# Where the weights' rounding copies and the softmax division run in the first groups of an attention and feed-forward kernel

## The chip, the cores and the metric

One NeuronCore of a Trainium2 chip runs the whole kernel. The metric is the device time of one execution in microseconds. Five engines work side by side, each with its own queue of instructions in a fixed order: TensorE (PE, its weight loads PEld), VectorE (DVE), ScalarE (ACT), GpSimd (POOL) and SyncE (SP), which issues nearly all transfers.

## What is computed

Attention with a local and a global window over 4 batches, 8 heads, 768 positions and 64 dimensions, then a feed-forward layer from 512 to 2048 and back.

```python
scores = scale * np.matmul(q, k.transpose(0, 1, 3, 2))
is_global = pos[None, :] < int(n_global)                 # 8
is_local = (rel >= 0) & (rel < int(n_local))             # 96
scores = np.where(is_global | is_local, scores + bias, -1000000000.0)
a = np.exp(scores - np.max(scores, axis=-1, keepdims=True))
a = a / (np.sum(a, axis=-1, keepdims=True) + 1e-09)
x = matmul(a, v)                                         # regrouped to 3072 rows of 512
h = x @ w_in                                             # w_in: 512 x 2048
g = np.where(h > 0.0, h, np.exp(np.minimum(h, 0.0)) - 1.0)
out = g @ w_out                                          # w_out: 2048 x 512
```

The two weight matrices arrive as 64-bit floats, as pairs of 32-bit words.

## The kernel before, in words

The 3072 rows are cut into 12 groups of 256 rows (`W`). Each group has four pairs of heads. For a pair, TensorE makes scores (`s`), DVE subtracts the distance table and takes the row maximum (L647, `pr`), ACT takes the exponential and sums it (L649), DVE adds 1e-9 and inverts the sums (`st`, L662 and L663), the scores are multiplied by the inverse (`norm`, by the helper `scaled`: L633 on ACT, L635 on DVE, L637 on POOL), TensorE transposes them (`t`), they are copied to SBUF (`pt`) and multiplied with the values (`pv`). The result is kept as a rounded part and a residual (`xh`, HI and LO). The groups 0 to 3 do this in `pair32`, where `norm` is called with `both=True`; the later groups do it in `pair`, with `both=False`.

The feed-forward layer has 16 blocks of 128 hidden units. TensorE makes `h` (L803), ACT and DVE make the ELU (`e`, L733 to L735), the result is rounded by ACT (`gh`) and its residual (`gl`) made by DVE or POOL, and TensorE multiplies it into the output (`o`, L763). Groups 0 to 2 go through the blocks in three segments, 0 to 4, 5 to 9 and 10 to 15, each for all three groups (`SEGS`). From group 3 on a scheme with seven products works on pairs of blocks (`a`, L880), with combinations of the second matrix's weights (`combos`, `g7`, L464, and `ta`, `tb`).

A weight block is prepared once, in `weight`, in the time of groups 0 to 2: SP loads the words (`bits`), ACT takes the absolute value of the high words (L433), DVE clamps, shifts and merges the words in four steps (L434, L438, L440, L442) into a 32-bit float (`g`), one copy rounds it to the type that TensorE reads (`w`, HI, by the helper `copy`: L336 on ACT, L338 on DVE and POOL), and one subtraction makes the residual (LO, L344, DVE or POOL). There are 32 such blocks, 16 of each matrix.

The order of all this work is not written by hand. Each operation is added to a `Plan` with a due time and a list of alternatives, each an engine, a cost in ns and whether it reserves the port that the planner lets DVE and POOL share. The planner runs through the work with these costs, and an operation goes to the engine where it would end first; what comes out is each engine's fixed queue. An operation that several engines may do is listed with several alternatives:

```python
def pool(n, two=True):
    return (("POOL", (30 + 2.58 * n) if two else (50 + 1.1 * n), True),)
```

`act`, `dve` and `pool` give these alternatives for n columns. A `dve` alternative reserves the port when it is marked fast or port.

Of the kernel before, what the change touches and what calls it, by code (L numbers as in the profile page):

```python
# [26 lines left out]
HI, LO = 0, 1  # L27
# [232 lines left out]
def act(n, psum=False, extra=0.0):  # L260
    return (("ACT", (55 if psum else 97) + 0.834 * n + extra, False),)


def dve(n, fast=False, port=False):
    return (("DVE", (75 + 0.521 * n) if fast else (70 + 1.042 * n), fast or port),)


def pool(n, two=True):
    return (("POOL", (30 + 2.58 * n) if two else (50 + 1.1 * n), True),)


def sp():
    return (("SP", 450.0, False),)


class Kernel:
# [136 lines left out]
    def weight(self, which, fc, due, after):  # L413
        nc, p, DM = self.nc, self.plan, self.DM
        tag = f"w{which}{fc}"
        bits = self.sb(tag, "bits", [P, 2 * DM], I32)
        g = self.sb("io", "g", [P, DM], I32)
        w = self.sb(tag, f"w{which}", [P, 2, DM], F32R)
        src = (self.w_in, self.w_out)[which][fc].bitcast(I32)
        words = lambda: bits.t.rearrange("p (n w) -> p n w", w=2)  # L420
        low, high = lambda: words()[:, :, 0], lambda: words()[:, :, 1]
        gf = lambda: g.t.bitcast(F32)

        def fetch(e):
            nc.sync.dma_start(bits.t, src)
            while self.values:
                self.values.pop(0)()

        load = p.add(sp(), fetch, writes=[bits], due=due - 9000, after=after, nbytes=P * DM * 8)
        if fc in self.ASKED:  # L430
            self.asked.append(load)
        if which in self.ABS:
            p.add((("ACT", 575.0, False),), lambda e: nc.scalar.activation(gf(), high().bitcast(F32), AF.Abs), [bits], [g], due - 6000)  # L433
            p.add(dve(DM, True), lambda e: nc.vector.tensor_scalar(gf(), gf(), F64_MIN, F64_MAX, ALU.max, ALU.min), [g], [g], due - 5500)  # L434
        else:
            p.add(dve(DM, port=True), lambda e: nc.vector.tensor_scalar(
                gf(), high().bitcast(F32), F64_MIN, F64_MAX, ALU.abs_max, ALU.min), [bits], [g], due - 5500)
        p.add(dve(DM, True), lambda e: nc.vector.tensor_scalar(g.t, g.t, 3, 0x3FFFFFFF, ALU.logical_shift_left, ALU.bitwise_and),  # L438
              [g], [g], due - 5000)
        p.add(dve(DM, port=True), lambda e: nc.vector.scalar_tensor_tensor(g.t, high(), -0x40000000, g.t, ALU.bitwise_and, ALU.bitwise_or),  # L440
              [bits, g], [g], due - 4500)
        p.add(dve(DM, port=True), lambda e: nc.vector.scalar_tensor_tensor(g.t, low(), 29, g.t, ALU.logical_shift_right, ALU.bitwise_or),  # L442
              [bits, g], [g], due - 4000)
        p.add(act(DM), lambda e: self.copy(e, w.t[:, HI], gf()), [g], [w], due - 3000)
        p.add(pool(DM) + dve(DM, port=True), lambda e: self.minus(e, w.t[:, LO], gf(), w.t[:, HI]),
              [g, w], [w], due - 2000)
        if which == 0 or fc < self.NF7:
            cols = slice(0, DM) if which == 0 else slice(DM // 2, DM)
            self.stores[which, fc] = p.add(sp(), lambda e: nc.sync.dma_start(self.kept[which][fc], w.t.bitcast(F32)[:, :, cols]), [w],
                                           due=due + self.KEEP, nbytes=P * DM * 8 // (1 + which), floor=self.KEEP)  # L450
        return w
# [30 lines left out]
    def pair(self, b, gi, hp, xh, xl, due, ahead, step, X):  # L482
# [41 lines left out]
        if rows:  # L524

            if "held" in X:
                self.loads += loads
            p.add((() if b == gi == 0 and hp < 3 else act(W) + dve(W, True)) + pool(W, False),
                  lambda e: self.scaled(e, q32(), q32(), sc), [rqv], [rqv], due - 9000)
            pv = self.bank("pv", "pv", [P, NT, P], X.get("pv"))  # L530
            self.pair32(b, hp, t0, q32, k32, v32, rqv, rk, pv, due, step, X)
            pvs = lambda: pv.t.rearrange("p i w -> p (i w)")
            p.add(act(W, True) + dve(W), lambda e: self.copy(e, xh.t[:, HI, hp], pvs()), [pv], [xh], due + 700)
            p.add(dve(W), lambda e: self.minus(e, xh.t[:, LO, hp], pvs(), xh.t[:, HI, hp]), [pv, xh], [xl], due + 800)
            if "held" in X:
                self.held += [o for v in (rqv, rk) for o in v.readers]
            return
# [132 lines left out]

    def norm(self, pr, lo, st, i, due, both):
        n = WN - lo
        more = act(n, extra=90) + pool(n, False) if both else act(n)
        self.plan.add(more + (("DVE", 130 + 0.53 * n, True),), lambda e: self.scaled(
            e, pr.t[:, lo:], pr.t[:, lo:], st.t[:, 2, i:i + 1]), [pr, st], [pr], due)

    def pair32(self, b, hp, t0, q32, k32, v32, rqv, rk, pv, due, step, X):
# [257 lines left out]
    def build(self):  # L935
# [46 lines left out]
        for fc, d in wdue.items():  # L982
            for which in range(2):
                def weight(which=which, fc=fc, d=d):
                    self.ws[which][fc] = self.weight(which, fc, d + 2 * which * self.STEP, self.loads + self.held if fc >= self.LATE else self.loads if fc > 1 else ())
                todo.append((first[fc] - 100.0, weight))
# [329 lines left out]
```

## Time and profile before

| | us |
|---|---|
| median of 3 runs | 657.6 (656.93 to 657.79) |
| the profiled execution, its own time | 655.9 |
| its span in the profile | 654.0 |
| busy in the span: PE, DVE, ACT, POOL | 641.9, 521.0, 478.1, 39.3 |
| POOL instructions in the span | 65 |

The profile is of one execution. An engine's busy time is the time in which it works on some instruction; the ends of matmuls are modelled, so a busy TensorE is not TensorE at its peak. The chain of work that ended last is followed back from the last instruction, at each step to what released it or to the instruction ahead of it on its engine. Rows of a group of instructions give the line, the engine, the operation, what is written and read with its shape, the count, the busy time and the mean length, and the idle time of the engine just before them.

### The profile page before, as it was taken

What the parts mean: (1) busy time and instruction counts of PE and PEld (TensorE: products, weight loads), DVE (VectorE), ACT (ScalarE), POOL (GpSimd) and SP (SyncE); (2) the same over time, 40 slices, a digit from 0 to 9 for tenths busy, and PEclk for the clock granted to TensorE, in tenths of its full rate; (3) what the DMA queues carried; (4) which work ended last, traced back from release to release, by engine and by line L of the source; (5) the groups of instructions that cost most, each with busy time, mean ns of one, the idle gap of its engine ahead of it and who ended that gap; (6) DMA issues with size and microseconds to landing.
All of it is one profiled execution on the core that took longest, in us unless ns stands there. A gap on an engine that the chain in (4) does not pass through costs nothing.

```text
span 654.0 us, 15999 instructions
## 1 busy us (share of the span) xinstructions
PE 641.9 (98%) x5950; PEld 599.0 (92%) x5950; DVE 521.0 (80%) x1510; ACT 478.1 (73%) x1243; POOL 39.3 (6%) x65
## 2 busy tenths in 40 slices
PE   8999999999999999999999999999999999999996
PEld 6677888888888999999999999999999999999996
DVE  7999999999998867866877786876777778766655
ACT  7998879766878777776777777776777777774442
POOL 4143101110211000000000000000000000000000
PEclk9999999999999999999999999999999999999999
DMA  8846996710237567657756756666775685575661
GB/s 272 302 119 221 365 361 248 275 65 13 73 112 262 191 215 241 237 190 233 254 190 213 274 180 223 237 234 202 229 263 181 222 284 187 178 250 174 216 204 36
DMA packets 52373, 137.71 MB, mean 211 GB/s; under 512 B 5698, under 2 KB 19010, under 8 KB 52290
## 3 DMA queue, kind: packets, MB, share of 16 engines
q1 hardware_dynamic: 52000, 136.37, 61.4%
q8 instruction: 48, 0.79, 0.5%
q14 instruction: 35, 0.29, 0.1%
q10 hardware_dynamic: 290, 0.26, 0.1%
HBM read 119.84 MB, written 16.78 MB: 209 GB/s over the span
## 4 chain that ended last, share of the span: by engine, by line
PE 83%; DVE 11%; ACT 3%; DMA 1%; issue 1%; POOL 0%; DVEq 0%; POOLq 0%; SPq 0%
PE h L803 36%; PE a L880 26%; PE o L763 6%; PE pv L614 4%; PE s L556 3%; PE t L576 3%; DVE g L464 2%; PE pv L725 1%; DMA rqv<-in_qkv_dram 1%; PE t L708 1%; ACT pr L649 1%; DVE gl L344 1%; PE s L691 1%; DVE e L735 1%; DVE g L440 1%
## 5 line engine op out<-in xcount | busy, mean ns | idle before, releaser
L803 PE MATMUL h<-xh,w0s 128*128 128x256 f32 x1728 | 203.1, 276 | 0.0
L803 PEld LDWEIGHTS h<-xh,w0s 128*128 128x128 f32 x1728 | 199.5, 188 | 0.1
L880 PE MATMUL a<-w,gg 128*128 128x256 f32 x864 | 143.5, 277 | 0.3 <-DVE xh L344 0.3
L336 ACT CAST gg<-z 128x384 fp32r<-128x384 f32 (+1 forms) x144 | 81.3, 565 | 70.4 <-DVE z L735 30.4
L735 DVE SCALAR_TENSOR_TENSOR z<-z,h 128x512 f32<-128x512 f32 x72 | 49.5, 687 | 95.2 <-ACT z L734 87.2
L880 PEld LDWEIGHTS a<-w,gg 128*128 128x128 f32 x864 | 120.3, 188 | 0.5 <-DVE xh L344 0.5
L649 ACT ACTIVATE pr<-pr,nmax 128x232 f32<-128x232 f32 (+1 forms) x192 | 90.0, 471 | 8.9 <-DVE nmax L647 8.5
L344 DVE TENSOR_TENSOR gg<-z,gg 128x512 fp32r<-128x512 f32 (+1 forms) x144 | 84.9, 618 | 7.4 <-ACT gg L336 6.6
L803 PEld LDWEIGHTS h<-xh,w 128*128 128x128 f32 x576 | 81.4, 189 | 8.9 <-issue 1.4
L803 PE MATMUL h<-xh,w 128*128 128x256 f32 x576 | 87.0, 283 | 0.1
L835 DVE TENSOR_TENSOR z<-z 128x128 f32<-128x128 f32 (+1 forms) x216 | 72.0, 333 | 5.2
L880 PE MATMUL a<-ta,gg 128*128 128x256 f32 x432 | 72.2, 276 | 0.0
L733 ACT ACTIVATE z<-h 128x512 f32<-128x512 f32 x72 | 42.9, 596 | 34.8 <-PE h L803 34.6
L647 DVE CUSTOM_DVE_ANT_0 pr<-s,tab 128x232 f32<-128x232 f32 (+1 forms) x192 | 63.4, 373 | 5.6 <-PE s L556 5.6
L763 PE MATMUL o<-w,gh 128*128 128x512 f32 x192 | 59.7, 403 | 1.5 <-DVE ob L790 1.2
L880 PEld LDWEIGHTS a<-ta,gg 128*128 128x128 f32 x432 | 59.7, 188 | 0.0
L880 PE MATMUL a<-tb,gg 128*128 128x256 f32 x216 | 50.0, 294 | 0.0
L734 ACT ACTIVATE z<-z 128x512 f32<-128x512 f32 x72 | 45.5, 632 | 1.8
L633 ACT ACTIVATE pr<-pr,st 128x232 f32<-128x232 f32 (+1 forms) x89 | 38.5, 468 | 9.4 <-DVE st L669 7.1
L763 PEld LDWEIGHTS o<-w,gh 128*128 128x128 f32 x192 | 32.0, 188 | 6.6 <-ACT pr L649 1.6
L880 PEld LDWEIGHTS a<-tb,gg 128*128 128x128 f32 x216 | 34.4, 188 | 3.8 <-issue 0.2
L649 ACT ACTIVATION_READ_ACCUMULATOR pr<-pr,nmax 128x1 f32 x192 | 36.8, 192 | 0.0
(129 smaller groups left out, 924.7 us busy)
## 6 DMA issues: line engine op xcount, KB each, us to landing
w0s<-kept SPq DMA_DIRECT2D x144, 512.0 KB, 5.0
rk<-in_qkv_dram SPq DMA_DIRECT2D x45, 184.0 KB, 2.5
bits<-in_w_in_dram SPq DMA_DIRECT2D x16, 512.0 KB, 6.2
bits<-in_w_out_dram SPq DMA_DIRECT2D x16, 512.0 KB, 9.2
kept<-w SPq DMA_DIRECT2D x16, 512.0 KB, 4.4
rv<-in_qkv_dram SPq DMA_DIRECT2D x32, 256.0 KB, 3.8
rqv<-in_qkv_dram SPq DMA_DIRECT2D x13, 384.0 KB, 3.5
rqv<-in_qkv_dram SPq DMA_DIRECT2D x34, 128.0 KB, 3.6
```

What stands on the lines that cost most here:

```text
L336: self.nc.scalar.copy(out, x)
L344: self.on(e).tensor_tensor(out, x, y, ALU.subtract)
L633: self.nc.scalar.activation(out, x, AF.Copy, scale=sc)
L647: p.add((("DVE", 158 + 1.042 * n, False),), lambda e: nc.vector.tensor_tensor_reduce(pr.t[:, lo:], st_()[:, lo:], tab, -(2.0 ** -(h + 1)), ...
L649: p.add(act(n, extra=200), lambda e: nc.scalar.activation(pr.t[:, lo:], pr.t[:, lo:], AF.Exp, bias=nm, scale=-1.0, accum_out=st.t[:, 0, i: ...
L733: p.add(act(n, True), lambda e: nc.scalar.activation(out(), hx(), AF.Relu, scale=-1.0), [h], [ex], due)
L734: p.add(act(n), lambda e: nc.scalar.activation(out(), out(), AF.Exp, scale=-1.0), [ex], [ex], due)
L735: p.add(dve(n), lambda e: nc.vector.scalar_tensor_tensor(out(), out(), -1.0, hx(), ALU.add, ALU.max), [h, ex], [ex], due)
L763: nc.tensor.matmul(acc[i].t, g.t[:, i * P:(i + 1) * P], w2.t[:, s], start=fc == f0 and n == 0 and s == HI, stop=fc == f1 - 1 and n == 1)
L803: self.nc.tensor.matmul(hx(), w1.t[:, s, cc * P:(cc + 1) * P], xh.t[:, x, cc], start=n == 0 and cc == 0, stop=n == 2 and cc == self.NCC - 1)
L835: tt = lambda e, out, x, y, op: self.on(e).tensor_tensor(out, x, y, op)
L880: nc.tensor.matmul(of[i].t[:, j], gg.t[:, x, g], w(s), start=first and x == s == 0 and (n in (0, 2, 4, 6) or final and n == 5), stop=last ...
```

## The change

In `weight` the rounding copy may go to POOL as well as to ACT, at a cost of its own (`cast`). In `norm` the calls with `both=True` (groups 0 to 3) may go to ACT or POOL, no longer to DVE; the calls with `both=False` are as before. POOL's cost for an operation with one input is 30 + 1.85 n instead of 50 + 1.1 n, and such an operation no longer reserves the port. Four lines are added ahead of everything the table below names, so a line of the new program stands 4 lower: L340, L342 are the copies, L348 the subtraction, L637, L639 and L641 the scalings on ACT, DVE and POOL.

```diff
--- before.py
+++ after.py
@@ -266,7 +266,11 @@
 
 
 def pool(n, two=True):
-    return (("POOL", (30 + 2.58 * n) if two else (50 + 1.1 * n), True),)
+    return (("POOL", (30 + 2.58 * n) if two else (30 + 1.85 * n), two),)
+
+
+def cast(n):
+    return (("POOL", 50 + 1.14 * n, False),)
 
 
 def sp():
@@ -441,7 +445,7 @@
               [bits, g], [g], due - 4500)
         p.add(dve(DM, port=True), lambda e: nc.vector.scalar_tensor_tensor(g.t, low(), 29, g.t, ALU.logical_shift_right, ALU.bitwise_or),
               [bits, g], [g], due - 4000)
-        p.add(act(DM), lambda e: self.copy(e, w.t[:, HI], gf()), [g], [w], due - 3000)
+        p.add(act(DM) + cast(DM), lambda e: self.copy(e, w.t[:, HI], gf()), [g], [w], due - 3000)
         p.add(pool(DM) + dve(DM, port=True), lambda e: self.minus(e, w.t[:, LO], gf(), w.t[:, HI]),
               [g, w], [w], due - 2000)
         if which == 0 or fc < self.NF7:
@@ -670,8 +674,8 @@
 
     def norm(self, pr, lo, st, i, due, both):
         n = WN - lo
-        more = act(n, extra=90) + pool(n, False) if both else act(n)
-        self.plan.add(more + (("DVE", 130 + 0.53 * n, True),), lambda e: self.scaled(
+        more = act(n, extra=90) + pool(n, False) if both else act(n) + (("DVE", 130 + 0.53 * n, True),)
+        self.plan.add(more, lambda e: self.scaled(
             e, pr.t[:, lo:], pr.t[:, lo:], st.t[:, 2, i:i + 1]), [pr, st], [pr], due)
 
     def pair32(self, b, hp, t0, q32, k32, v32, rqv, rk, pv, due, step, X):
```

What the planner makes of it, over the whole program: 15 of the 32 rounding copies of 512 columns are on POOL instead of none, 17 on ACT. Of the divisions of 232 columns DVE has 14 fewer, ACT 11 more and POOL 3 more; of those of 128 columns ACT has 2 fewer and POOL 2 more. Of the scalings of rqv DVE has 3 fewer, ACT 1 and POOL 2 more. Of the 512-column residuals of weights POOL has 8 instead of 5. TensorE's real work is the same, in another order up to about its 1150th instruction and in the same order from there.

POOL's queue, in the first group's softmax. `pr` are the exponentials of one head and tile, `st` the inverse sums, `w0_99` the first block of the first matrix, `g` its float. Before:

```order
L637 TENSOR_SCALAR pr_32_215<-pr_32_215,st_36_226 128x128
L637 TENSOR_SCALAR pr_33_218<-pr_33_218,st_36_226 128x232
L637 TENSOR_SCALAR pr_46_262<-pr_46_262,st_50_267 128x128
L637 TENSOR_SCALAR pr_48_275<-pr_48_275,st_50_267 128x128
L637 TENSOR_SCALAR pr_60_381<-pr_60_381,st_64_385 128x128
L637 TENSOR_SCALAR pr_62_387<-pr_62_387,st_64_385 128x128
L637 TENSOR_SCALAR pr_63_404<-pr_63_404,st_64_385 128x232
L637 TENSOR_SCALAR pr_74_426<-pr_74_426,st_78_445 128x232
```

and now:

```order
L641 TENSOR_SCALAR pr_32_213<-pr_32_213,st_36_226 128x128
L641 TENSOR_SCALAR pr_34_228<-pr_34_228,st_36_226 128x128
L342 CAST w0_99_318<-g_98_238 128x512
L641 TENSOR_SCALAR pr_46_273<-pr_46_273,st_50_290 128x128
L641 TENSOR_SCALAR pr_47_288<-pr_47_288,st_50_290 128x232
L641 TENSOR_SCALAR pr_48_292<-pr_48_292,st_50_290 128x128
L641 TENSOR_SCALAR pr_49_298<-pr_49_298,st_50_290 128x232
L348 TENSOR_TENSOR w0_105_359<-g_104_300,w0_105_359 128x512
```

The copy of the first weight block stands between the divisions of the first group, and a residual of another weight follows.

ACT's queue, where the first segment's weights meet the second group's exponentials. Before:

```order
L649 ACTIVATE pr_77_451,st_78_445<-pr_77_451,nmax_98 128x232
L336 CAST w1_102_483<-g_101_300 128x512
L336 CAST xh_1_308<-pv_57_474 128x256
L633 ACTIVATE pr_75_431<-pr_75_431,st_78_445 128x232
L633 ACTIVATE pr_77_451<-pr_77_451,st_78_445 128x232
L649 ACTIVATE pr_88_481,st_92_509<-pr_88_481,nmax_98 128x232
L433 ACTIVATE g_110_517<-bits_109_392 128x512
```

and now, from the same exponential:

```order
L653 ACTIVATE pr_77_453,st_78_437<-pr_77_453,nmax_98 128x232
L340 COPY pt_68_474<-t_67_457 116x256
L653 ACTIVATE pr_88_492,st_92_496<-pr_88_492,nmax_98 128x232
L637 ACTIVATE pr_76_441<-pr_76_441,st_78_437 128x232
L653 ACTIVATE pr_89_494,st_92_496<-pr_89_494,nmax_98 128x232
L437 ACTIVATE g_110_524<-bits_109_414 128x512
```

The copy of `w1_102` has gone to POOL and the rounding of `xh_1` to DVE, and another division stands there.

DVE's queue, from the last step that makes the float of the first weight (L442, now L446) to its residual. Before:

```order
L442 SCALAR_TENSOR_TENSOR g_98_238<-bits_97_176,g_98_238 128x512
L344 TENSOR_TENSOR xh_1_308<-pv_15_281,xh_1_308 128x256
L662 TENSOR_SCALAR st_50_267<-st_50_267 128x4
L663 RECIPROCAL st_50_267<-st_50_267 128x4
L338 COPY pt_40_316<-t_39_304 116x256
L635 TENSOR_SCALAR pr_49_289<-pr_49_289,st_50_267 128x232
L344 TENSOR_TENSOR w0_99_320<-g_98_238,w0_99_320 128x512
```

and now:

```order
L446 SCALAR_TENSOR_TENSOR g_98_238<-bits_97_176,g_98_238 128x512
L348 TENSOR_TENSOR xh_1_308<-pv_15_280,xh_1_308 128x256
L438 TENSOR_SCALAR g_104_300<-g_104_300 128x512
L342 COPY pt_40_316<-t_39_304 116x256
L348 TENSOR_TENSOR w0_99_318<-g_98_238,w0_99_318 128x512
```

The rounding copy of `w0_99` lies between the first and the last of these rows, on ACT before and on POOL now; one division and the reciprocal have left the piece.

## Rows read from the trace of the kernel before

**Rows 1.** The chain of work that ended last, by line: 0 to 62, 62 to 124, 124 to 190, 190 to 654 us

```profile
by line: DMA rqv<-in_qkv_dram 11.4%; ACT pr L649 9.9%; PE t L708 7.9%; PE pv L725 6.7%; PE o L763 6.4%; PE s L691 6.2%; issue 5.0%; PE h L803 4.5%; ACT pt L336 3.5%; POOL pr L637 3.3%; DVE pr L647 3.2%; ACT g L433 2.7%; DVE gl L344 2.4%; PE
by line: PE o L763 41.5%; PE h L803 41.4%; PE pv L725 7.6%; PE t L708 5.4%; PE s L691 4.2%; DVE e L735 0.7%; issue 0.0%
by line: DVE g L464 16.7%; DVE gl L344 8.4%; DVE e L735 8.1%; DVE g L440 7.1%; issue 6.3%; DVE w L344 5.9%; DVE g L442 5.6%; PE o L763 5.0%; DMA rqv<-in_qkv_dram 4.0%; PE h L803 3.9%; DVE part L780 3.6%; DVE pr L647 3.3%; DVE ta L344 3.1%; 
by line: PE h L803 43.6%; PE a L880 37.2%; PE pv L614 5.8%; PE s L556 4.8%; PE t L576 3.7%; PE o L763 1.7%; DVE gg L344 0.5%; PE th L576 0.2%; DVE z L835 0.2%; DVE fin L905 0.2%; DVE z L735 0.1%; issue 0.1%; ACT z L734 0.1%; DVE xh L344 0.1
```

**Rows 2.** Busy time by stretch and engine, in us (instructions), TensorE's granted clock, DMA

```profile
0.00:62.00 62.00, 56.63 (x424) 43.90 (x424) 57.52 (x218) 52.76 (x167) 20.22 (x40) 1.00 0.66 218
62.00:124.00 62.00, 62.00 (x448) 53.95 (x447) 59.88 (x159) 52.73 (x138) 7.99 (x12) 1.00 0.88 335
124.00:190.00 66.00, 64.57 (x430) 55.53 (x431) 65.86 (x168) 46.56 (x131) 9.10 (x10) 1.00 0.17 55
190.00:654.00 464.00, 458.67 (x4655) 445.64 (x4653) 337.76 (x969) 326.08 (x809) 2.03 (x3) 1.00 0.65 215
sum 654.00, PE 641.86 PEld 599.02 DVE 521.02 ACT 478.13 POOL 39.35; mean PE 160.47 PEld 149.76 DVE 130.25 ACT 119.53 POOL 9.84
```

**Rows 3.** ACT's groups by shape, 0 to 215 us: busy us, mean ns, idle before

```profile
L336 ACT CAST w<-g 128x512 fp32r<-128x512 f32 x32 | 19.9, 620 | 2.9 <-DVE g L442 2.8
L633 ACT ACTIVATE pr<-pr,st 128x232 f32<-128x232 f32 x18 | 8.5, 489 | 1.1 <-DVE st L663 1.0
```

**Rows 4.** ACT in order of time: start us, length us

```profile
25.63 0.61 ACT L336 CAST w<-g 128x512 fp32r<-128x512 f32 x1
26.14 0.37 ACT L336 CAST xh<-pv 128x256 fp32r<-128x256 f32 x1
```

**Rows 5.** POOL's scaling, line L637: ns min/median/max, first and last start

```profile
L637 POOL TENSOR_SCALAR pr<-pr,st x32: 364/459/1168, 8.9 to 169.8; 128x232 f32<-128x232 f32 x21, 128x128 f32<-128x128 f32 x11
L637 POOL TENSOR_SCALAR rqv<-rqv,scale x6: 478/478/924, 3.2 to 76.1; 128x256 f32<-128x256 f32 x6
```

**Rows 6.** POOL's groups by shape, 0 to 215 us

```profile
L344 POOL TENSOR_TENSOR w<-g,w 128x512 fp32r<-128x512 f32 x5 | 6.5, 1294 | 30.3 <-ACT w L336 30.2
```

**Rows 7.** DVE's scaling, line L635: ns min/median/max

```profile
L635 DVE TENSOR_SCALAR pr<-pr,st x71: 280/340/545, 8.8 to 582.8; 128x232 f32<-128x232 f32 x65, 128x128 f32<-128x128 f32 x6
L635 DVE TENSOR_SCALAR rqv<-rqv,scale x6: 341/351/1074, 16.5 to 127.7; 128x256 f32<-128x256 f32 x6
```

**Rows 8.** DVE in order of time, around the marks

```profile
83.18 0.41 DVE L735 SCALAR_TENSOR_TENSOR e<-e,h 128x256 f32<-128x256 f32 x1
83.51 0.68 DVE L442 SCALAR_TENSOR_TENSOR g<-bits,g 128x512 int32<-128x512 int32 x1
...
124.00 0.41 DVE L735 SCALAR_TENSOR_TENSOR e<-e,h 128x256 f32<-128x256 f32 x1
...
190.62 0.41 DVE L735 SCALAR_TENSOR_TENSOR e<-e,h 128x256 f32<-128x256 f32 x1
```

**Rows 9.** DVE and POOL in order of time, at four places

```profile
58.14 0.60 POOL L637 TENSOR_SCALAR pr<-pr,st 128x232 f32<-128x232 f32 x1 [5.24 <-DVE st L663]
58.17 0.71 DVE L635 TENSOR_SCALAR pr<-pr,st 128x232 f32<-128x232 f32 x2
...
75.96 0.68 DVE L442 SCALAR_TENSOR_TENSOR g<-bits,g 128x512 int32<-128x512 int32 x1
76.06 0.92 POOL L637 TENSOR_SCALAR rqv<-rqv,scale 128x256 f32<-128x256 f32 x1 [5.82 <-PE h L803]
...
142.96 1.29 POOL L464 TENSOR_TENSOR g<-w 128x512 f32<-128x512 f32 x1 [4.63 <-DVE w L344]
143.13 1.67 DVE L440 SCALAR_TENSOR_TENSOR g<-bits,g 128x512 int32<-128x512 int32 x1
...
185.75 0.95 DVE L344 TENSOR_TENSOR tb<-g,tb 128x256 fp32r<-128x256 f32 x1
```

## The prediction

> **What bounds the kernel now.** Begin with the chain of work that ended last, cut into four stretches [rows 1]. From 62 to 124 us it is TensorE alone (h, o, pv, t and s make up all but 1%). From 124 to 190 us it is mostly DVE: combinations of weights (g L464), residuals (gl, w, ta L344), unpacking (g L440, L442). From 190 us to the end it is TensorE again, and its order there is the same in both programs. Ahead of 62 us it is mixed: ACT's exponentials, loads of rqv, DVE's and POOL's softmax steps, short pieces of TensorE. The second view, busy time by stretch, says how full the helpers are [rows 2]. By its sum TensorE looks busy for 642 of 654 us and DVE for 521, as if TensorE were the bound everywhere; but the ends of matmuls are modelled, and stretch by stretch DVE works 57.5 of the first 62 us and 65.9 of the 66 us of the third, ACT 52.8 and 46.6, POOL 20.2 and 9.1. So time can be won or lost in the first and third stretch only, and POOL is the engine with room. TensorE's granted clock is 1.00 (the 2.4 GHz level) throughout and plays no part.
>
> **The change, part by part.** Three edits to the planner's alternatives.
>
> (1) The rounding copy of a weight (ACT, 0.620 us, 32 times [rows 3]) may go to POOL; the new order has 15 of 32 there. No row shows POOL copying 512 columns. It scales 256 columns in 0.478 us and, at the least, 128 in 0.364 [rows 5]: 0.9 ns a column, so by an estimate from these rows 0.71 us for 512. The bounds are 0.478 (half the columns) and 1.294 (two inputs, 512 columns [rows 6]); I take 0.71, since scaling has one input like the copy. On ACT the next instruction starts 0.51 us after such a copy [rows 4]. So a weight comes 0.1 to 0.2 us later, and ACT is relieved of 15 x 0.51 = 7.7 us.
>
> (2) The softmax division (`norm`) of the first four groups loses DVE: 14 leave DVE's order, all of 232 columns; ACT gets 11 more of these and 2 fewer of 128, POOL 3 more and 2 more. One lasts 0.340 us on DVE [rows 7]; DVE's instructions overlap by 0.08 (0.41 long, the next 0.33 later [rows 8]), so it is worth 0.26. On ACT it is worth 0.39 (0.489 less 0.10 of overlap [rows 3, 4]).
>
> (3) POOL's one-input work is priced at 30 + 1.85 n instead of 50 + 1.1 n, and no longer reserves the port that the planner lets POOL and DVE share. For 232 columns that is 459 instead of 305 ns; the median row is 459 [rows 5]. The new price is right, the freedom is the danger: the planner now lays POOL's copies beside any work of DVE.
>
> The rest follows from the planner's balance: POOL gets three more 512-column residuals, DVE some evacuations from ACT. Loads and stores stay on SP, 738 instructions in both; some key and query loads change places by a few rows.
>
> For the sum I use marks that both programs pass. **Mark one** is the ELU of the third group's first hidden block (L735, at 83.18 us [rows 8]), when the softmax of groups 0 to 2 is done. Counted along DVE's order, there stand ahead of it 10 norms and 2 scalings of rqv fewer (0.26 and 0.27, from 0.351 [rows 7]), one w residual and one L440 fewer (0.60 each), and more, each at the spacing of its kind: one gl, one xh cast, one 116x256 copy (0.34 each), one 116x512 copy (0.60), two 128-column copies (0.21): -2.6 - 0.5 - 1.2 + 2.0 = -2.3 us. On ACT: nine copies fewer (-4.6), six norms and one rqv more (+2.7), five evacuations and one unpacking fewer (-1.9): -3.8 us. The later engine counts, DVE: -2.3. Against it stand nine POOL copies ahead of that mark. What does one cost DVE? At 58.14 POOL scales for 0.60 us, and the two DVE norms beside it take 0.71 together where 0.26 + 0.34 = 0.60 was due: DVE loses 0.11, POOL 0.14. At 76.06 POOL takes 0.92 instead of 0.478 behind DVE's L442, which keeps its 0.68: DVE loses nothing [rows 9]. I take the middle of 0 and 0.11, 0.06 a copy: +0.5. Stretch one: -1.8 us.
>
> The Trainium skill (SBUF — State Buffer, "Who interferes with whom") speaks against this edit: the port pair is an exclusive lock, and a DVE instruction with two SBUF inputs, or in a two-port mode, blocks fully behind a POOL instruction that reads SBUF. Taken to its end, each copy could hold DVE for its whole length, and the change would lose time (third rival). The row of 143.13 agrees, for two-input POOL work; that of 76.06 shows the lock falling the other way.
>
> **Mark two** spans DVE's stretch, from the ELU at 124.00 to that at 190.62 [rows 8]. The same count gives -3.1 ahead of the first and -3.9 ahead of the second, so 0.8 us less within. Three copies lie here: +0.2. POOL's two-input steps grow here from seven to nine. The first of the seven made L440 last 1.67 us instead of 0.68, the last a tb residual 0.95 instead of 0.42 [rows 9]; over the seven DVE's excess is 3.4 us, 0.48 each: +1.0. Stretch three: +0.4. The second stretch hides what happens in it (TensorE is fed), the fourth is unchanged. Sum: -1.8 + 0.4 = **-1.4 us**.
>
> The change adds a wait: in nine of 15 cases the residual behind a POOL copy is on DVE, three to eight instructions after the last unpacking step. If the copy is late, everything in DVE's queue behind that residual waits: xh residuals, ELUs, and with them TensorE. For w0_99 three instructions cover it, 0.34 each, 1.0 us: 0.3 more than the copy. Without that cover the excess is DVE's loss, which is how the third rival comes about.
>
> The profiled execution took 655.9 us, 1.9 more than its span; the median of the runs shown is 657.6, 1.7 above it. From the median: 657.6 - 1.4 = 656.2.
>
> **The rivals.** *Relief in full.* The copies cost DVE nothing, as at 76.06, and stretch one shortens by ACT's 3.8; stretch three gives 0.8: 657.6 - 4.6 = 653.0. For it: exponentials (pr L649) and evacuations (pt L336) of ACT stand high in the first stretch's chain, and the first segment's ELUs move forward. Against it: 58.14. Chance 0.18.
>
> *The gain is hidden.* The planner spends the relief on weights and pulls the first group's output products forward, while the reciprocals of groups 1 and 2 mostly come 1 to 2.4 us later in DVE's count than before; these open the next segments. Stretch one then gives nothing, stretch three +0.4: 658.0. For it: TensorE's unbroken second stretch, where what is ready early only queues. Chance 0.22.
>
> *Slower: POOL's copies hold up DVE.* Twelve copies stand ahead of mark one and in stretch three, where DVE mostly has two-input or two-port work. At 0.40 us each (between 0.06 and the whole 0.71) stretch one is -2.3 + 3.6 = +1.3, stretch three -0.8 + 1.2 + 1.0 = +1.4: 660.3. Without copies the sum is -2.1, so it decides from 0.18 us a copy (no gain) and is plainly slower from 0.28. For it: 143.13, and that the plan no longer keeps the two apart; against it: 58.14 and 76.06. Chance 0.25.
>
> **How the numbers follow.** A measurement of this kernel can tell about 0.2%, 1.3 us, from no change. The forecast, -1.4, has 0.35; its own range is 654.5 to 657.7, so some 0.22 of it counts as faster, 0.13 as within. Relief in full is faster (0.18); the hidden gain is 0.02 faster, 0.16 within, 0.04 slower; the third rival slower (0.25). Together: faster 0.42, within 0.29, slower 0.29. The range runs from just under full relief to just over the third rival, 652.4 to 660.5; a lock at its whole 0.71 us, 664, is left out.
>
> **What would show it.** Right: POOL casts of about 0.7 us; the means of DVE's L440 and L344 rows no longer than now; the third group's first ELU some 2 us earlier, and everything from 190 us on shifted by the same amount, otherwise unchanged. Wrong: POOL casts of 1 us and more, DVE idle ahead of w residuals with POOL named as the releaser, or L440 and L344 means longer by tens of ns (third rival); the mark at 83 us unmoved, with more idle time on ACT (second). If the chain behind 190 us held much besides TensorE, the division into stretches would be wrong.

## The result and the profile after

The changed kernel takes 661.72 us (median of 6 runs, 661.22 to 663.06) against 656.82 us for the kernel before on the same chip (6 runs, 655.78 to 657.79): ratio 1.0077, 95% interval 1.0066 to 1.0087. It is 4.9 us slower where 1.4 us less was forecast, and outside the range. The profiled execution took 661.22 us, with a span of 659.4.

First the marks of [rows 8], in DVE's order of time: the third group's first ELU, and the ELUs at the two ends of the third stretch.

```profile
86.98 0.41 DVE L739 SCALAR_TENSOR_TENSOR e<-e,h 128x256 f32<-128x256 f32 x1
...
129.65 0.41 DVE L739 SCALAR_TENSOR_TENSOR e<-e,h 128x256 f32<-128x256 f32 x1
...
195.10 0.41 DVE L739 SCALAR_TENSOR_TENSOR e<-e,h 128x256 f32<-128x256 f32 x1
```

Against 83.18, 124.00 and 190.62 before, they come 3.80, 5.65 and 4.48 us later. So the part ahead of mark one lost 3.80 us (its neighbours at 80.64 and 86.92 come 1.25 and 2.95 later, so "about 3" is the safer reading), the part from there to the next mark lost 1.85 (42.67 us instead of 40.82), the third stretch won 1.17, and the rest lost 0.77 in its first 15 us and then ran alongside: the last residual of the program starts at 650.93 instead of 645.68, 5.25 later. Lateness at the first marks is not yet loss at the end. One of the kernels below, price_only, passes mark one 2.46 us and the ELU of 124.00 1.97 us later than the kernel before, that of 190.62 0.90 us sooner, and is faster.

Then the chain of waits, cut at 62, 124 and 190 us (three of the four stretches) as in [rows 1]:

```profile
by line: DMA rk<-in_qkv_dram 11.8%; ACT pr L653 10.9%; PE t L712 5.1%; issue 4.3%; PE s L695 4.0%; ACT pr L637 4.0%; SPq L429 3.7%; ACT pt L340 3.6%; PE pv L729 3.3%; DVE g L444 3.2%; DVE w L348 3.2%; PE o L767 3.1%; DVE pr L651 3.1%; DVE g
by line: PE h L807 29.9%; PE o L767 27.5%; PE t L712 5.6%; DMA kept<-w 5.5%; PE pv L729 5.3%; DVE g L444 4.6%; PE s L695 3.9%; DVE part L784 1.9%; DVE st L666 1.9%; DVE g L446 1.9%; POOL pr L641 1.5%; DVE g L438 1.2%; DVE g L442 1.2%; DVE e
by line: PE h L807 22.3%; PE o L767 21.3%; DVE g L444 7.5%; DVE w L348 7.2%; DVE e L739 5.8%; DVE g L446 5.7%; issue 5.3%; DVE gl L348 4.9%; DVE g L442 4.3%; DVE g L438 4.2%; DVE part L784 3.6%; PE pv L729 2.4%; DVE g L468 2.2%; PE t L712 2
```

The second row is the news. Before, the second stretch was TensorE and 0.7% of ELU; now DVE's unpacking of weights (g L444, L446, L438, L442), a softmax step of 4 columns (st L666) and a store (kept) stand in it. The store held nothing up: DVE was not idle ahead of the step at 110.49 us that it is said to have released. The third row went the other way: TensorE now leads a stretch that had been DVE's.

Busy time by stretch, as in [rows 2]:

```profile
0.00:62.00 62.00, 56.25 (x404) 41.70 (x406) 54.29 (x200) 47.88 (x152) 28.71 (x49) 1.00 0.58 192
62.00:124.00 62.00, 60.80 (x426) 51.69 (x423) 58.85 (x152) 50.21 (x135) 16.69 (x19) 1.00 0.90 336
124.00:190.00 66.00, 64.71 (x436) 56.20 (x435) 65.89 (x164) 44.16 (x121) 16.58 (x18) 1.00 0.23 78
```

In the first 62 us DVE works 3.2 us less than before and ACT 4.9 less. Up to mark one itself, where the prediction counted, DVE is busy for 76.3 us instead of 77.4 and ACT for 68.9 instead of 71.4, and DVE stands idle for 10.7 us instead of 5.8. So the relief is there, and the mark does not come sooner. In the second stretch TensorE, which never paused, now pauses for 1.2 us, and the list of its waits there, empty before, has one row (us in total, times, longest):

```profile
PE h L807 <- DVE e L739: 1.0, 1, 1.0
```

POOL's copies, and its groups by shape from 0 to 215 us (beside [rows 5] and [rows 6]):

```profile
L342 POOL CAST w<-g x15: 610/741/1627, 14.7 to 156.6; 128x512 fp32r<-128x512 f32 x15
```

```profile
L342 POOL CAST w<-g 128x512 fp32r<-128x512 f32 x15 | 12.7, 849 | 48.6 <-DVE g L446 21.2 <-ACT gh L340 18.3 <-ACT xh L340 5.7
L348 POOL TENSOR_TENSOR w<-g,w 128x512 fp32r<-128x512 f32 x8 | 10.4, 1298 | 3.6 <-ACT w L340 3.1
```

A copy takes 0.61 us at the least, 0.74 at the median and 0.85 at the mean, where 0.71 was estimated. What it does to DVE shows in DVE's groups from 8 to 205 us. First the kernel before, then the changed one:

```profile
L440 DVE SCALAR_TENSOR_TENSOR g<-bits,g 128x512 int32<-128x512 int32 x32 | 22.6, 712 | 0.0
L434 DVE TENSOR_SCALAR g<-g 128x512 f32<-128x512 f32 x32 | 13.3, 416 | 0.8 <-ACT g L433 0.8
L662 DVE TENSOR_SCALAR st<-st 128x4 f32<-128x4 f32 x16 | 3.1, 191 | 1.5 <-ACT pr L649 1.5
```

```profile
L444 DVE SCALAR_TENSOR_TENSOR g<-bits,g 128x512 int32<-128x512 int32 x32 | 23.9, 748 | 0.1
L438 DVE TENSOR_SCALAR g<-g 128x512 f32<-128x512 f32 x32 | 15.1, 478 | 1.6 <-ACT g L437 1.6
L666 DVE TENSOR_SCALAR st<-st 128x4 f32<-128x4 f32 x16 | 4.9, 305 | 0.3 <-ACT pr L653 0.2
```

The same instructions in the same number are 36, 62 and 114 ns longer. The first of these is a sign that the prediction named for its third rival. Two others that it named hardly show, as the row of the weights' residuals (L344 before, 680 ns) says:

```profile
L348 DVE TENSOR_TENSOR w<-g,w 128x512 fp32r<-128x512 f32 x24 | 16.4, 684 | 0.5 <-POOL w L342 0.5
```

They last 4 ns more, and DVE waited only 0.5 us in all ahead of them for a copy to be finished. So that the copies come late is a small part at most.

Where DVE's time is lost is seen in POOL's and DVE's order of time around 115 us (POOL first):

```profile
114.52 0.61 POOL L342 CAST w<-g 128x512 fp32r<-128x512 f32 x1
115.21 1.29 POOL L348 TENSOR_TENSOR w<-g,w 128x512 fp32r<-128x512 f32 x1
118.59 0.74 POOL L342 CAST w<-g 128x512 fp32r<-128x512 f32 x1 [2.08 <-DVE g L446]
119.41 1.35 POOL L348 TENSOR_TENSOR w<-g,w 128x512 fp32r<-128x512 f32 x1
```

```profile
115.40 1.66 DVE L444 SCALAR_TENSOR_TENSOR g<-bits,g 128x512 int32<-128x512 int32 x1
...
118.78 0.83 DVE L438 TENSOR_SCALAR g<-g 128x512 f32<-128x512 f32 x1
119.53 1.26 DVE L666 TENSOR_SCALAR st<-st 128x4 f32<-128x4 f32 x1
```

Each of the three starts 0.12 to 0.19 us behind a POOL instruction and ends only after it: POOL's residual of 115.21 ends at 116.50 and L444 at 117.06; the copy of 118.59 ends at 119.33 and L438 at 119.61; the residual of 119.41 ends at 120.76, and L666, a step on four columns that takes 0.16 us alone, at 120.79. In 5 us DVE loses 1.66 - 0.68, 0.83 - 0.41 and 1.26 - 0.16: 2.5 us.

Summed over 8 to 205 us (each DVE instruction that overlaps a POOL instruction: its length less the median of its shape with none beside it, put down to the POOL instruction that overlaps it most), POOL cost DVE 6.5 us before and 10.4 after: 2.8 beside the 15 copies (0.19 each), 1.7 beside one-input steps, 5.8 beside two-input steps. Of the second stretch alone it was 0.3 us before and is 4.7 now, 3.0 of it beside two-input steps.

Which of DVE's steps are held is plain in seven traces (before, after, kept_act, kept_act_beside, mid_act, first_act, mid_res_dve), again from 8 to 205 us. Take the DVE steps that start behind a POOL step which had more than 0.25 us to go and was not itself held (at most 0.06 us over the shortest of its shape). Unpacking and combinations of weights (g), the residuals gl, ks and tb, scalings and the 128x4 step (st, L666) were held 71 times of 71, for what was left of POOL's step less 0.12 to 0.20 us; in the three above, 1.10, 0.55 and 1.23 us were left. The scores' maximum, ELUs, xh residuals and copies of t, which read what TensorE wrote, and reciprocals were held 0 times of 340.

### The profile page after: what moved, and what is told of

It reads as the page before. It is cut to its first block, busy times and chain, and to the rows that moved or that the text cites. A ratio compares the mean times of both kernels' runs of the same rounds, so it can differ in the third digit from the quotient of the medians.

```text
span 659.4 us, 16020 instructions
## 1 busy us (share of the span) xinstructions
PE 645.7 (98%) x5950; PEld 599.6 (91%) x5950; DVE 520.5 (79%) x1494; ACT 473.6 (72%) x1232; POOL 66.6 (10%) x92
## 4 chain that ended last, share of the span: by engine, by line
PE 82%; DVE 10%; ACT 3%; DMA 2%; issue 1%; SPq 1%; POOL 1%; DVEq 0%; POOLq 0%
PE h L807 36%; PE a L884 26%; PE o L767 7%; PE pv L618 4%; PE s L560 4%; PE t L580 3%; DVE g L444 1%; PE t L712 1%; DMA rk<-in_qkv_dram 1%; DVE w L348 1%; PE pv L729 1%; ACT pr L653 1%; DVE g L446 1%; DVE e L739 1%; DVE g L438 1%
## 5 line engine op out<-in xcount | busy, mean ns | idle before, releaser
L340 ACT CAST gg<-z 128x384 fp32r<-128x384 f32 (+1 forms) x144 | 81.3, 565 | 70.5 <-DVE z L739 30.4
L348 DVE TENSOR_TENSOR gg<-z,gg 128x512 fp32r<-128x512 f32 (+1 forms) x144 | 84.9, 618 | 7.4 <-ACT gg L340 6.6
L651 DVE CUSTOM_DVE_ANT_0 pr<-s,tab 128x232 f32<-128x232 f32 (+1 forms) x192 | 63.2, 374 | 6.0 <-PE s L560 5.9
L637 ACT ACTIVATE pr<-pr,st 128x232 f32<-128x232 f32 (+1 forms) x98 | 41.9, 469 | 11.4 <-DVE st L673 7.2
```

The lines of the kernel that those rows point to most:

```text
L340: self.nc.scalar.copy(out, x)
L348: self.on(e).tensor_tensor(out, x, y, ALU.subtract)
L637: self.nc.scalar.activation(out, x, AF.Copy, scale=sc)
L651: p.add((("DVE", 158 + 1.042 * n, False),), lambda e: nc.vector.tensor_tensor_reduce(pr.t[:, lo:], st_()[:, lo:], tab, -(2.0 ** -(h + 1)), ...
```

## The experiments

Sixteen kernels ran, each timed against the kernel before on the same chip; a "+" below is the ratio's excess times 656.8 us. The changed kernel stands at +5.1.

**One edit at a time.** Three kernels with the norm edit, the copy edit or the price alone, and one with the first two together. Each is the diff of the section on the change, cut to one or two of its three pieces.

```diff
-        more = act(n, extra=90) + pool(n, False) if both else act(n)
-        self.plan.add(more + (("DVE", 130 + 0.53 * n, True),), lambda e: self.scaled(
+        more = act(n, extra=90) + pool(n, False) if both else act(n) + (("DVE", 130 + 0.53 * n, True),)
+        self.plan.add(more, lambda e: self.scaled(
```

> Only the norm edit, on the kernel before: the softmax division may go to ACT or POOL, no longer to DVE; POOL keeps its old prices, copies stay on ACT. Theory EARLY (the new POOL prices set another order on ACT in the first 15 us: the abs of a second early weight, which waits for its load, comes to stand ahead of the exponentials of the third pair, worth some 3 us there): ACT's early order is that of before, the third pair's reciprocal stays within 1 us of its time before, total 656 to 657.5. Theory HOLD (POOL's copies, and the two-input residuals right behind them, hold up DVE between 105 and 140 us): no copies, so 656 to 657.5 too. Theory NORM (the division off DVE lengthens the softmax chain itself): the reciprocal of the third pair 3 us later, total 659 to 661.

657.56 us, ratio 1.0015 (1.0004 to 1.0026): +1.0, just above the range of EARLY and HOLD. The third pair's reciprocal comes at 15.81 us instead of 14.62, a little more than EARLY's 1 us. NORM asked for 3 us there and 659 at the least; it falls.

```diff
-        p.add(act(DM), lambda e: self.copy(e, w.t[:, HI], gf()), [g], [w], due - 3000)
+        p.add(act(DM) + cast(DM), lambda e: self.copy(e, w.t[:, HI], gf()), [g], [w], due - 3000)
```

> Only the copy edit, on the kernel before: the weights' rounding copies may go to POOL (11 of 32 do), prices and division as before. EARLY: early order as before, so no 3 us at 15 us; total 656 to 657.5. HOLD: each POOL copy costs DVE 0.2 to 0.4 us ahead of 140 us, so 658.5 to 660.5. NORM: no difference, 656 to 657.5.

668.97 us, ratio 1.0207 (1.0181 to 1.0233): +13.6, more than any theory gave. The ELU of 83.18 comes 5.1 us later and that of 190.62 comes 4.7 later; the rest comes behind 190 us, where no copies are (last section).

```diff
-    return (("POOL", (30 + 2.58 * n) if two else (50 + 1.1 * n), True),)
+    return (("POOL", (30 + 2.58 * n) if two else (30 + 1.85 * n), two),)
```

> Only the new price of POOL's one-input work (30 + 1.85 n, the shared port not reserved), on the kernel before; no copies on POOL, DVE may still divide. EARLY: the second early weight's abs stands ahead of the third pair's exponentials on ACT, their reciprocal comes 3 us later, and some 1.5 to 3 us of it reach the end: 658.5 to 660. HOLD: without copies little is held, 656 to 658. NORM: 656 to 657.5.

655.32 us, ratio 0.998 (0.9965 to 0.9995): -1.3, the fastest of all kernels tried. The early mark did come late (16.87 instead of 14.62), but the reciprocals that stand at 40.20 and 50.03 us before come 0.02 and 1.45 us sooner, and the ELU of 190.62 comes 0.90 sooner. EARLY's price for that place falls. The prediction called this edit's "freedom" the danger because copies could then lie beside any work of DVE. This run has no copies, so it shows only that the freedom costs nothing without them; the copies have theirs from `cast`, which cast_port below changes.

> The changed kernel without the new price: copies on POOL (14) and the division off DVE, POOL's one-input work priced and kept apart from DVE as before. EARLY: early order as before, so the 3 us at 15 us are gone and the total falls to 656 to 658.5. HOLD: the copies still hold up DVE, 659 to 661.5, about as slow as the changed kernel. NORM: still 3 us at 15 us, 660 to 662.

660.42 us, ratio 1.0056 (1.0037 to 1.0074): +3.7, inside HOLD's range and above EARLY's. It is inside NORM's too, but the third pair's reciprocal comes at 15.36 us, not 3 us late. Without the copies, norm_only, it was +1.0. So the copy edit costs, with or without the other two; how much of that is the copies and how much the new order, the next runs tell.

**The copies taken away, the order kept.** A new plan differs at many places, so a sharper cut leaves every engine's order as it is and moves the copies alone from POOL to ACT as the program is written out.

```diff
-                op.emit(op.eng)
+                op.emit('ACT' if len(op.alts) == 2 and op.alts[1] == cast(self.DM)[0] and op.eng == 'POOL' else op.eng)
```

> The order of the changed kernel kept instruction for instruction on every engine; only the 15 copies that it gives to POOL are issued on ACT, each at the place in the program where POOL had it. Theory HOLD (a copy running on POOL takes DVE's time beside it): the hold is gone, some 3 of the 4.9 us come back, 657.5 to 659.5. Theory LATE (the copy itself comes too late on POOL, behind POOL's own queue and 0.12 us slower, and the residual and all of DVE behind it waits): also gone, 657.5 to 659.5, unless ACT's queue makes it later still. Theory ORDER (the new order of the other steps, made because the planner thinks ACT relieved, is what loses; who copies matters little): 661 to 663, with ACT's 7.7 us of copies back even above that.

660.06 us, ratio 1.0041 (1.0027 to 1.0055): +2.7. That lies between HOLD's range and ORDER's, and both have a part: 2.4 us of the 5.1 are the copies on POOL, and 2.7 remain with the order and the copies on ACT. POOL costs DVE 5.4 us here from 8 to 205 us instead of 10.4, and 1.5 instead of 4.7 in the second stretch. The two marks, in DVE's order of time:

```profile
86.88 0.42 DVE L739 SCALAR_TENSOR_TENSOR e<-e,h 128x256 f32<-128x256 f32 x1
...
127.21 0.42 DVE L739 SCALAR_TENSOR_TENSOR e<-e,h 128x256 f32<-128x256 f32 x1 [0.16 <-ACT e L738]
```

Mark one stands where the changed kernel has it (86.98). Between the marks lie 40.33 us instead of 42.67: all of the 2.3 us come back there, and the chain of the second stretch is TensorE alone again:

```profile
by line: PE h L807 42.0%; PE o L767 40.2%; PE pv L729 6.6%; PE t L712 6.5%; PE s L695 4.8%
```

POOL's residual that had started at 115.21 starts at 113.80 here, and L444 beside it takes 0.98 us instead of 1.66.

In the next run POOL gets other work at those places (`junk` is an 80-column tile that nothing else uses, `cp` the condition above; cut: the tile is filled once, and the copy itself goes to ACT as in the last run):

```diff
+                if cp:
+                    for _ in range(2):
+                        self.nc.gpsimd.tensor_copy(self.junk.t, self.junk.t)
```

> As the last one (the changed kernel's order, the 15 copies on ACT), and POOL does work for nobody where it had each copy: two copies of an 80-column tile onto itself, some 0.6 us together, that nothing waits for except POOL's own next step. HOLD: DVE is held by that work as by the copies, so the time of the changed kernel is back, 660.5 to 662.5, 2 to 3 us above the run without it. LATE: nobody needs that work, so only POOL's own next steps come later; within 1 us of the run without it. ORDER: within 1 us of the run without it, both at 661 or more.

661.02 us, ratio 1.0057 (1.0042 to 1.0072): +3.7, 1.0 us above the run without that work where HOLD asked for 2 to 3 and LATE for less than 1, with intervals that overlap. The time decides nothing. Its trace is plainer: 41.46 us between the marks (88.13 and 129.59), 1.1 of the 2.3 us lost again; the two L445 there (L444 in the changed kernel) take 1.49 and 1.77 us, each beside a two-input residual that this work had pushed back. It supports HOLD and speaks against LATE, since no copy is late here: the copies are on ACT.

**Without copies, and with copies kept apart**, each planned anew.

```diff
-        p.add(act(DM) + cast(DM), lambda e: self.copy(e, w.t[:, HI], gf()), [g], [w], due - 3000)
+        p.add(act(DM), lambda e: self.copy(e, w.t[:, HI], gf()), [g], [w], due - 3000)
```

> The changed kernel without the copy edit: division off DVE and the new POOL price, copies on ACT, planned anew. HOLD and LATE: no copies on POOL, so no more than the two other edits alone gave (+1.1 and -1.1): 655.5 to 658. ORDER: 655.5 to 658 as well, since the planner no longer counts on a relieved ACT; it is told apart by the two runs before.

658.78 us, ratio 1.0028 (1.0017 to 1.0039): +1.8, 0.8 us above the range that all three theories gave.

```diff
-    return (("POOL", 50 + 1.14 * n, False),)
+    return (("POOL", 50 + 1.14 * n, True),)
```

> The changed kernel, but a copy on POOL reserves the port that the planner lets POOL and DVE share (8 of 32 copies are then on POOL). HOLD: the planner keeps copies and DVE's two-port work apart, so little is held: 657 to 659. LATE: the copies come no sooner, half as many: 658.5 to 660.5. ORDER: ACT is relieved by half as much, 658.5 to 660.5.

660.09 us, ratio 1.004 (1.0025 to 1.0055): +2.6, above HOLD's range and inside the others'. With copies that the plan keeps apart the loss is about half, but there are 8 of them instead of 15, so this run does not tell keeping apart from having fewer.

**The early place again.** In the changed kernel ACT waits 0.99 us for the load of a weight while the third pair's exponentials stand behind it. ACT's steps on weights (L437), in order of time:

```profile
9.42 0.67 ACT L437 ACTIVATE g<-bits 128x512 f32<-128x512 f32 x1 [0.53 <-POOL pr L641]
...
12.91 0.70 ACT L437 ACTIVATE g<-bits 128x512 f32<-128x512 f32 x1 [0.99 <-DMA bits<-in_w_out_dram]
```

That pair's reciprocal comes at 18.21 us instead of 14.62. A floor in the plan puts this step behind them, first in the kernel without copies. ORDER-EARLY says that this place makes what the order costs, ORDER-SPREAD that lateness arises at many places:

```diff
-            p.add((("ACT", 575.0, False),), lambda e: nc.scalar.activation(gf(), high().bitcast(F32), AF.Abs), [bits], [g], due - 6000)
+            p.add((("ACT", 575.0, False),), lambda e: nc.scalar.activation(gf(), high().bitcast(F32), AF.Abs), [bits], [g], due - 6000, floor=15300.0 if (which, fc) == (1, 0) else 0.0)
```

> Division off DVE and new POOL price, no copies on POOL, with the same floor. ORDER-EARLY: its 1.8 us above before are gone, 656 to 657.5. ORDER-SPREAD: still 658 to 660.

657.14 us, ratio 1.0007 (0.9998 to 1.0016): the reciprocal is back at 15.04 and 1.4 us of the 1.8 are gone. Without copies ORDER-EARLY's forecast comes true, though the floor also made a new plan.

> The changed kernel with one floor: the abs of the second early weight (w_out's first) may not be planned before 15.3 us, so on ACT it comes to stand behind the exponentials of the third pair; planned anew, 18 copies on POOL. Theory ORDER-EARLY (the 2.7 us that are left without copies on POOL come from that place: the exponentials wait behind an abs that waits for its load, and the lateness is never made up): the third pair's reciprocal is back within 1 us of before, TensorE's loss at 15 to 25 us is gone, total 1.5 to 2.7 us under the changed kernel, 659 to 660.5. Theory ORDER-SPREAD (lateness arises at many places, since every division now queues on ACT or POOL; the early place is made up by 60 us): the early mark is mended, the total within 1 us of the changed kernel, 661 to 663.

663.48 us, ratio 1.0111 (1.0095 to 1.0127): the reciprocal is nearly back (15.73), and the time is worse, +7.3, with 18 copies on POOL. ORDER-EARLY fails for the changed kernel, and the loss is above ORDER-SPREAD's range too.

> The same order kept, with its 18 copies issued on ACT in their places. ORDER-EARLY with HOLD: both causes gone, 656.5 to 658. ORDER-SPREAD with HOLD: 2 to 2.5 us under the run before it, 659 to 660.5.

662.49 us, ratio 1.0078 (1.0062 to 1.0093): +5.1, outside both ranges. By the ratios 2.2 us come back (1.0 by the medians); the order that was planned for 18 copies on POOL does badly on ACT too.

> Only the new POOL price, with the same floor: the version that could beat both kernels. ORDER-EARLY: the price edit alone was 1.3 us under before though its early mark was 2.2 us late; with that mended 654 to 655.5. ORDER-SPREAD: as without the floor, 655 to 656.

656.25 us, ratio 0.9991 (0.9982 to 1.0): -0.6, no better than the price edit without the floor, and above the ranges of both theories, though the reciprocal is back (14.65 instead of 16.87).

**Where the copies cost it.** Again the changed kernel's order, kept; only some of the copies, or the residuals behind two of them, change engine.

```diff
-                op.emit(op.eng)
+                early = len(op.alts) == 2 and op.alts[1] == cast(self.DM)[0] and op.eng == 'POOL' and 60000 < op.start < 123000
+                op.emit('ACT' if early else op.eng)
```

> The changed kernel's order kept; only the five copies between 62 and 124 us are issued on ACT, the other ten stay on POOL. Theory MIDDLE (what the copies cost is lost at 107 to 124 us, where DVE has no slack and TensorE waits for its ELUs; held DVE time ahead of that is made up): all of the 2.2 us come back, 658.5 to 660. Theory EVERYWHERE (each copy costs about the same 0.15 us to the end): a third of it comes back, 660.5 to 661.5.

658.67 us, ratio 1.0032 (1.002 to 1.0044): +2.1. Five copies give back all that 15 gave.

```profile
87.55 0.42 DVE L739 SCALAR_TENSOR_TENSOR e<-e,h 128x256 f32<-128x256 f32 x1
...
127.87 0.42 DVE L739 SCALAR_TENSOR_TENSOR e<-e,h 128x256 f32<-128x256 f32 x1 [0.16 <-ACT e L738]
```

40.32 us between the marks. In the next run the condition is `op.start < 60000`.

> The changed kernel's order kept; only the seven copies ahead of 62 us are issued on ACT, eight stay on POOL. MIDDLE: next to nothing comes back, 661 to 662.5. EVERYWHERE: half of it, 660 to 661.

662.76 us, ratio 1.0088 (1.0071 to 1.0104): +5.8, nothing comes back.

```profile
89.46 0.41 DVE L739 SCALAR_TENSOR_TENSOR e<-e,h 128x256 f32<-128x256 f32 x1
...
132.12 0.42 DVE L739 SCALAR_TENSOR_TENSOR e<-e,h 128x256 f32<-128x256 f32 x1
```

42.66 us between the marks, as in the changed kernel. EVERYWHERE falls; MIDDLE holds, its range passed by 0.3 us on the slow side (mark one is late by a fall of the clock, last section).

```diff
-                op.emit(op.eng)
+                late = op.eng == 'POOL' and len(op.alts) == 2 and op.alts[0] == pool(self.DM)[0] and op.writes[0].name[:2] in ('w0', 'w1') and 105000 < op.start < 123000
+                op.emit('DVE' if late else op.eng)
```

> The changed kernel's order kept, copies on POOL; only the two weight residuals that POOL starts right behind its copies at 114.5 and 118.6 us are issued on DVE, each at its place in the program. If the residuals hold DVE there (L444 at 115.40 took 1.66 us instead of 0.68, the L666 at 119.53 1.26 instead of 0.16: 2.1 us in all, against 1.2 us of DVE for doing them): about 1 us comes back, 660 to 661. If the copies themselves do it: no gain or 1 us worse, 661.5 to 663.

660.61 us, ratio 1.0052 (1.0035 to 1.0068): +3.4, 1.7 us under the changed kernel, with 41.80 us between the marks. DVE does 1.2 us of work more there and is still faster: L444 is back at 0.69 us and L666 at 0.15, and only L438 beside the copy stays long:

```profile
118.40 0.83 DVE L438 TENSOR_SCALAR g<-g 128x512 f32<-128x512 f32 x1
119.15 0.15 DVE L666 TENSOR_SCALAR st<-st 128x4 f32<-128x4 f32 x1
```

So of the 3.0 us that the five copies cost, somewhat more than half is not beside the copies but beside the residuals that POOL starts right behind two of them.

> The copy edit alone, its order kept, with its 11 copies issued on ACT. Its marks were 4.7 us late at 190 us, and from there to the end its matmuls followed one another at 116 to 117.5 ns instead of 113 to 114, 7.5 us more. If POOL's copies hold DVE: 1 to 3 us come back ahead of 190 us, 666 to 668. If all of it is the order planned for the copies: 668 to 670. The slower matmuls lie where POOL has no copies; if they stay, they belong to the order or the places of tiles, if they go, to the copies: 660 to 662.

666.29 us, ratio 1.0147 (1.0127 to 1.0166): +9.7, inside the range for copies that hold DVE. The copies on POOL cost 4 us there; the remaining 9.7 belong to that kernel's order, the slower matmuls behind 190 us among them.

## Why the prediction was wrong

**The bound and the fourth stretch: right but for 0.8 us.** They are lost between 190 and 206 us; from there the two programs run alongside, 5.3 us apart.

**Step (1), the copies: the mechanism of the third rival, with its place and form missed.** The copy's own time was near (0.71 against 0.74 at the median). The step "I take the middle of 0 and 0.11, 0.06 a copy" failed. Beside the copies DVE lost 0.19 us each, and the middle of two cases was the wrong form: a meeting costs DVE nothing when its instruction started first (as at 75.96 us in [rows 9]) or reads what TensorE wrote, and otherwise nearly the rest of POOL's instruction (0.42 beside the copy of 118.59, 0.98 and 1.10 beside the residuals). Of two steps that need the same ports, the Trainium skill says which one waits ("Issue order, not op shape, decides who blocks.", SBUF — State Buffer, "Who interferes with whom"); these three rows agree. The working priced the copy and left out what stands behind it on POOL: a copy of 0.6 us puts off POOL's two-input residual, and where that then falls decides 1 us each time. The kept-order runs show it: five copies, or the two residuals behind them, give 3.0 and 1.7 us back. That the third rival's sum, 660.3, came near the measured time is luck: it had 0.40 us a copy, twice what was lost beside one, and no loss in the second stretch.

**"The second stretch hides what happens in it (TensorE is fed)": wrong.** It lost 1.85 us; with its five copies on ACT it is 0.5 us shorter than before (40.32 against 40.82). DVE was busy for 59.9 of its 62 us [rows 2]; TensorE's unbroken row in the chain of before showed that nothing was late, and not that there was room. The third rival counted the copies "ahead of mark one and in stretch three" and so left out three of the five that decided, the ones at 105.79, 114.52 and 118.59 us.

**Step (2), the relief of stretch one: counted too high, and not turned into time.** Up to mark one DVE was busy for 1.1 us less and ACT for 2.5 less (DVE's held time included), where -2.3 and -3.8 were counted, but the mark came about 3 us later and not 1.8 sooner. DVE's idle time ahead of the mark grew by 4.9 us, four times what its work shrank: it waited, so work taken from it there did not shorten the stretch. The hidden-gain rival saw the place ("the reciprocals of groups 1 and 2 mostly come 1 to 2.4 us later") and took it for harmless. For the kernel without copies the abs put ahead of the third pair's exponentials costs 1.4 us, as far as a new plan can show. In price_only the same floor gave nothing, and in the changed kernel, where it came with a new plan and 18 copies, the time was worse; the abs alone was not moved in the changed kernel's own order, so what it costs there is not shown.

**Stretch three: wrong sign, to the good.** The two-input steps were to cost 0.48 us each; from 124 to 205 us DVE lost 1.8 us beside them instead of 3.4, though 11 of them start between the two marks where nine were counted, and the stretch was 1.2 us shorter, not 0.4 longer. The smaller loss may not be all of it: price_only, late at mark one too, was 2.9 us shorter there (63.75 instead of 66.62).

**What stays open.** With no copy in the second stretch 2.1 us are left (mid_act), and about as much without any copies (no_cast). In the latter 1.4 us of it may be the early place; what it is in the former was not isolated, but for a part that may go with the clock (last section). No version with copies on POOL came out below the kernel before; the price edit alone did, by 0.2%, at the edge of what can be told.

## What to carry to other kernels

When work moves to POOL, price not its length but its meetings with DVE. In these traces a DVE step of the kinds above that starts second waits nearly to the end of POOL's, so look at what stands behind the moved step on POOL, and at how little idle time DVE has there. A stretch in which the chain shows TensorE alone may still have no room: look at the busy time of the engine that feeds it. And taking work off a busy engine saved no time here, since it left that engine waiting for others. To tell the two causes apart, keep the order and move the one step.

## What was not expected of the hardware

In the copy edit alone, matmuls followed one another more slowly through the whole rest of the program, with no pause and the granted clock at 1.00. Groups of TensorE from 240 to 420 us, the kernel before and then the copy edit alone:

```profile
L803 PE MATMUL h<-xh,w0s 128*128 128x256 f32 x704 | 82.4, 276 | 0.0
```

```profile
L807 PE MATMUL h<-xh,w0s 128*128 128x256 f32 x672 | 80.9, 280 | 0.0
```

From start to start that is 117.0 ns instead of 113.6 at the mean, and the part from the ELU of 190.62 to the last residual is 7.6 us longer. DVE's and ACT's steps there keep their lengths (L647 and L651, the scores' maximum, 392 and 394 ns). It stays when the copies go back to ACT (cast_only_act: 280 and 117.0 ns too), so it is not the copies' engine. That kernel's order and the places of its tiles are left; which, is open. The changed kernel doesn't have it (276 and 113.6 ns).

In some executions of the changed kernel's order the granted clock falls below 1.00 at about 20 us, after TensorE was busy for 2.5 of 4 us: in first_act's profile

```profile
16.00:20.00 4.00, 2.49 (x22) 1.32 (x20) 3.19 (x9) 3.56 (x13) 0.49 (x1) 1.00 0.31 97
20.00:24.00 4.00, 3.39 (x15) 2.49 (x11) 2.74 (x14) 2.15 (x8) 3.10 (x5) 0.62 0.33 108
```

and its 0.62 is a mean over a stretch that has both levels (2.4 and 1.2 GHz). The changed kernel's own profile shows 2.46 us of TensorE from 16 to 20 us and no fall. Its runs with a mean clock of 0.996 took 661.8 to 663.1 us, those with 0.998 and 0.999 661.2 to 661.7, so about 1 us goes with it. A difference of up to 1 us between two medians above may therefore be partly the clock's. For instance, mid_act's three runs with 0.995 to 0.997 took 659.7 to 659.9 us, its other eight 657.7 to 659.5, and five of kept_act's six had 0.997, which may be why kept_act stands 0.6 us above mid_act. The times between marks used above lie behind it.
